# Attention pairs 4 and 5 moved to the padded, DMA-transposed form in a fused state-space and gated-FFN kernel

## The chip, the cores and the metric

The kernel runs on one core of one Trainium2 chip. The metric is the device time of one launch in microseconds (us), taken as the median of several runs. TensorE multiplies matrices, VectorE and ScalarE empty its results from PSUM, GpSimd works on SBUF alone, and SyncE issues most of the DMAs. In the profile they are PE (PEld for its weight loads), DVE, ACT, POOL and SP. An engine with a small q behind its name is its instruction queue, which issues DMAs.

## The reference

Two layers stand behind each other. The first is a chunked state-space attention over 4 batches, 8 heads, 768 positions, head width 32 and state width 16:

```python
# per batch and head, chunk by chunk
cum = cumsum(log a);  L = exp(cum_i - cum_j), causal
y  = ((C @ B.T) * L) @ x          # inside a chunk ("intra")
y += exp(cum) * (C @ state)       # from earlier chunks ("inter")
state = decay * state + sum_j B_j x_j * decay_from_j
```

The second takes `y` as 3072 tokens of width 256 through a gated FFN with 1536 hidden columns: `out = (relu(y @ w_gate) * (y @ w_val)) @ w_out`. Inputs and output are float32; the kernel multiplies in bfloat16.

## The kernel before

The attention works on 12 pairs of 128-position chunks (three pairs to a batch), the FFN on 6 blocks of 512 tokens. Block b of the FFN needs pairs 2b and 2b+1. While block b is computed, the attention of the next two pairs, called P = 2b+2 and Q = 2b+3 in the code, is slipped between its matmuls; W = 2b+1 is the pair before. The order on every engine is the order of the text: `in_order` ties each instruction to the one before it on its engine, so an engine that waits holds up all that stands behind it in the text.

A pair goes through these steps. `load_bc` and `load_x` issue its DMAs from SP: C, B and x, two DMAs each. GpSimd scales B and C by the decays and casts x (`to_x`). TensorE needs B and C with positions along the free axis. Then come the scores (`G`, `G_rows`), which ScalarE, VectorE and GpSimd copy out and mask (`gevac`; `causal` is GpSimd's part of the mask, on what ScalarE has copied), the product of the scores with x (`Dm`, `Dm_two`), the part from earlier chunks (`inter`, `inter_rows`) and the copy of both to `yT`, from which the FFN reads. The chunk states are built up in one PSUM tile, `A_ps`.

There are three forms of a pair:

- Pairs 0 to 3 are "wide": the even and odd positions of a chunk pair are interleaved. `scale_bc` writes B and C to `bs`, TensorE transposes them (`turn`), ScalarE and VectorE copy the result (`tevac`).
- Pairs 4 and 5 (`p < NDMA`, line 283) go through `scale_bc` and `turn` as well, without the interleaving. Their states come from `states` and `spread`, which keep a state in a 128x256 masked form `Sm` for one matmul of full height.
- Pairs 6 to 11 are "padded": `scale_padded` writes B and C with zeros between into one of three buffers `bz`, and SP issues a DMA transpose into `TT`. TensorE does nothing for it. States come from `states_two` for two pairs at once and are summed by `sums_two` (VectorE adds, GpSimd makes the masked copy `Sn`); `inter_rows` multiplies them in tiles of 32 rows.

The FFN part of a block has 12 hidden slices. `gv` computes one for 512 tokens, `gvh` for 256 at a time: the second half of a block's tokens comes from pair W, and a block can start on the first half before pair W is done. The number of slices done in halves is `nh`: 4 in block 0 (ahead of the loop), 6 in block 1, 8 in block 2, none later. In the middle of the halves for the first 256 tokens stands pair W's last part. Then `fout` multiplies the 12 slices by `w_out` for four groups of 128 tokens (`ts` 0 to 3), and the attention of P and Q goes between these.

For blocks 2 and later the stretch of `fout` holds, in this order on TensorE: 9 slices, `G_rows(P)`, both `inter_rows`, 16 more slices, `G_rows(Q)`, 19 slices, `Dm_two((P, Q))`, `states_two` of the two pairs after, 4 slices.

Of the kernel before, what the change touches and what calls it, by code (L numbers as in the profile page):

```python
# [8 lines left out]
FP32 = mybir.dt.float32  # L9
# [20 lines left out]
def kernel(  # L30
# [70 lines left out]

    def load(p, q):
# [12 lines left out]
    even = const.tile([128, 24], FP32)  # L115
# [137 lines left out]
    over2 = const.tile([128, NB], FP32)  # L253
# [6 lines left out]
    def over_sum(de):  # L260
        own = smask.rearrange("p t (q d) -> p (t q) d", q=4)[:, :, 0]
        prod = const.tile([128, NB, 8], FP32)
        nc.vector.tensor_tensor(
            out=prod, in0=de.rearrange("p (b h) -> p b h", b=NB),
            in1=own.rearrange("p (o h) -> p o h", o=1).to_broadcast([128, NB, 8]),
            op=ALU.mult)
        nc.vector.tensor_reduce(out=over, in_=prod, op=ALU.add, axis=mybir.AxisListType.X)

    def over_sum2(de):
        own = smask.rearrange("p t (q d) -> p q t d", q=4)[:, :, :, 0]  # L270
        prod = const.tile([128, 2, 8], FP32)
        for n in range(2):
            nc.vector.tensor_tensor(
                out=prod[:, n].rearrange("p (q t) -> p q t", t=2),
                in0=de[:, (2 + n) * 8:(3 + n) * 8].rearrange("p (q t) -> p q t", t=2),
                in1=own, op=ALU.mult)
        nc.vector.tensor_reduce(out=over2[:, 2:4], in_=prod, op=ALU.add,
                                axis=mybir.AxisListType.X)
# [4 lines left out]
    NDMA = 6  # L283
# [8 lines left out]
    def scale_padded(p, eng):  # L292
# [11 lines left out]
        st[p]["B"] = [z[:, 4 * i] for i in range(2)]  # L304
        tt = st[p]["TT"] = att.tile([128, 8, 128], BF16, tag="TT", name="TT", bufs=4)
        nc.sync.dma_start_transpose(out=tt, in_=z.rearrange("s k n -> s (k n)"))

    def new_bs(p):
        st[p]["bs"] = att.tile([128, 4, 128], BF16, tag="bs", name="bs", bufs=6)
        bs = st[p]["bs"]  # L310
        if p < NWIDE:
            st[p]["tin"] = [[bs[:, 2 * j + r] for r in range(2)] for j in range(2)]
        else:
            st[p]["tin"] = [[bs[:, 2 * i + j] for i in range(2)] for j in range(2)]
            st[p]["B"] = st[p]["tin"][0]
# [4 lines left out]
    def views(p, js):  # L320
        s = st[p]
        dst = s["bs"].rearrange("s k (q t n) -> s k t q n", q=4, t=2)
        if p < NWIDE:
            ks = slice(2 * js.start, 2 * js.stop)
            src = s["bcr"].rearrange("s (t q) j r n -> s (j r) t q n", t=2)
            return src[:, ks], dst[:, ks]
        return s["bcr"].rearrange("s i j (t q) n -> s (i j) t q n", t=2), dst

    def cast_bc(p, eng, js):
        src, dst = views(p, js)  # L330
        for t in range(2):
            copy(eng, dst[:, :, t], src[:, :, t])

    def scale_bc(p, eng, js=slice(0, 2), f=None, ts=(0, 1)):
        b, c0, _ = place(p)
        src, dst = views(p, js)
        if f is None:
            if p < NWIDE:
                f = wfac[:, p, js].rearrange("s j r h -> s (j r) h")
            else:  # L340
                f = fac[:, b, c0:c0 + 2].rearrange("s c j h -> s (c j) h")
        n = f.shape[1]
        for t in ts:
            eng.tensor_tensor(  # L344
                out=dst[:, :, t], in0=src[:, :, t],
                in1=f[:, :, 4 * t:4 * t + 4].to_broadcast([128, n, 4, N]), op=ALU.mult)

    def scale_one(p, eng, j):

        b, c0, _ = place(p)  # L350
        for i in range(2):
            f = fac[:, b, c0 + i, j].rearrange("s (t q) -> s t q", t=2)
            eng.tensor_tensor(
                out=st[p]["bs"][:, 2 * i + j].rearrange("s (q t n) -> s t q n", q=4, t=2),
                in0=st[p]["bcr"][:, i, j].rearrange("s (t q) n -> s t q n", t=2),
                in1=f.to_broadcast([128, 2, 4, N]), op=ALU.mult)

    def to_x(p, eng, f=None):
        xb = att.tile([128, 2 * NH * D], BF16, tag="xb", name="xb", bufs=6)
        xr = st[p]["xr"].rearrange("s i h d -> s (i h) d")  # L360
        out = xb.rearrange("s (k d) -> s k d", d=D)
        if f is None:
            copy(eng, out, xr)
        else:
            eng.tensor_tensor(out=out, in0=xr, in1=f.to_broadcast([128, 2 * NH, D]),
                              op=ALU.mult)
        st[p]["x"] = [xb[:, i * NH * D:(i + 1) * NH * D] for i in range(2)]

    def scale(p, eng):
        if p >= NDMA:  # L370
            scale_padded(p, eng)
        else:
            new_bs(p)
            scale_bc(p, eng)
        to_x(p, eng)
# [15 lines left out]
    def bevac(p, eng):  # L391
# [3 lines left out]
        if p < NWIDE:  # L395
            src = src.rearrange("s r m -> s m r")
            dst = dst.rearrange("s (m r) -> s m r", r=2)
        else:
            src = src.rearrange("s i m -> s (i m)")
        copy(eng, dst, src)  # L400
# [16 lines left out]
    def ct(p, i, rows=slice(0, 128), t=None):  # L417
        if p < NWIDE:
            c = st[p]["CT"][rows, :, :, 64 * i:64 * i + 64]
        else:  # L420
            c = st[p]["CT"][rows, :, i]
        return c if t is None else c[:, t]

    def split(p, ap):

        return ap.rearrange("s t (r m) -> s t r m", r=2) if p < NWIDE else ap
# [17 lines left out]
    def G(p):  # L444
# [4 lines left out]
        for i in range(2):  # L449
            for q in range(4):  # L450
                r = slice(32 * q, 32 * q + 32)
                nc.tensor.matmul(  # L452
                    out=split(p, g[q][:, i]), lhsT=s["BT"][r, i], rhs=ct(p, i, r),
# [100 lines left out]
    chunks = {}  # L554

    def states(p):
        c0 = 2 * (p % PPB)
        last = c0 + 2 == NC
        chunks[p] = (st[p]["B"], st[p]["x"])
        todo = [(0, p, 0)]  # L560
        if c0 and not last:
            todo.insert(0, (0, p - 1, 1))
        if not last:
            todo += [(1, p, 0), (1, p, 1)]
        for n, (k, e, i) in enumerate(todo):
            B_, x_ = chunks[e]
            xi = x_[i].rearrange("s (t q d) -> s q t d", t=2, q=4)
            for q in range(4):
                nc.tensor.matmul(
                    out=A_ps[0][32 * q:32 * q + 32, 0, 64 * k:64 * k + 64].rearrange(  # L570
                        "p (t d) -> p t d", t=2),
                    lhsT=B_[i][:, 32 * q:32 * q + 32], rhs=xi[:, q],
                    start=(n == 0 and (c0 == 0 or last)), stop=True,
                    tile_position=(0, 32 * q),
                    skip_group_check=True)

    def spread(p):
        for k in range(1 if 2 * (p % PPB) + 2 == NC else 2):
            S[2 * p + k + 1] = spread_one(2 * p + k + 1, k)

    def y_bank(s, apart=False):
        if "y" not in s:
# [4 lines left out]
            else:  # L587
                y = mm.tile([128, 2, 2, 128], FP32, tag="y", name="y")
                s["y"] = [y[:, 0], y[:, 1]]
                s["ya"] = y  # L590
# [8 lines left out]
    def inter(p, i):  # L599
# [5 lines left out]
        for t in range(2):  # L605
# [10 lines left out]
            out = s["y"][t][:, i]  # L616
            if p < NWIDE:
                out = out.rearrange("s (r m) -> s r m", r=2)
            nc.tensor.matmul(  # L619
                out=out, lhsT=Sm[:, t], rhs=ct(p, i, t=t),  # L620
# [16 lines left out]
    def yevac(p, *engs):  # L637
        s = st.pop(p)
        dst = yT[:, :, p * 256:(p + 1) * 256]
        if p >= NWIDE:  # L640
            copy(engs[0], dst.rearrange("q t (i m) -> q t i m", i=2), s["ya"])
            return
# [14 lines left out]
    def inter_rows(p, opened):  # L657

        for i in range(2):
# [3 lines left out]
            for q in range(4):  # L663
# [5 lines left out]
                opened.add(q)  # L669

# [29 lines left out]
    def sums_two(ps):  # L700

        A = A_ps[0].rearrange("p a d -> p (a d)")
        for n, (p, i) in enumerate(todo(ps)):
            c = 2 * p + i
# [96 lines left out]
    def foevac(b, ts, o=None):  # L801
# [10 lines left out]
        rows = out[r0 - 128:r0 + 128, :].rearrange("(i p) m -> p i m", p=128)  # L812
        for part in ((slice(0, 1), slice(1, 2)) if b in (2, 3) and ts == 3 else (slice(0, 2),)):
            nc.sync.dma_start(out=rows[:, part], in_=ob[:, part])
# [116 lines left out]
    de = const.tile([128, BH], FP32)  # L931
# [21 lines left out]
    nc.scalar.copy(out=de, in_=de_ps)  # L953
# [9 lines left out]
    for b in range(NBLK):  # L963
        P, Q, W = 2 * b + 2, 2 * b + 3, 2 * b + 1
        more = P < NPAIR
        if b == 1:
            load(P + 2, nc.sync)
            load(P + 3, nc.sync)
        if b == 2:
            scale(Q, nc.gpsimd)  # L970
            load(Q + 2, nc.sync)

        nh = (4, 6, 8, 0)[min(b, 3)]
        for f in range(nh):
            if b == 0:
                continue
            turning = f == (3 if b == 1 else nh - 3)
# [3 lines left out]
            if b == 1 and f == 1:  # L981
                to_x(P, nc.scalar)
            if turning:
                inter(W, 0)
                inter(W, 1)
                Dm(W)
                if b == 1:
                    states(P)
# [167 lines left out]
```

## Time and profile before

| | |
|---|---|
| median of 3 runs (lowest to highest) | 122.64 us (122.54 to 122.77) |
| the profiled execution's own time | 122.54 us |
| its span in the profile | 120.8 us |
| PE busy in the span | 116.8 us (97%) |
| DVE, ACT, POOL busy | 89.2, 74.3, 51.4 us |
| DMA queue of SP (q1) | 73088 packets, 10.54 MB |
| DMA transposes (`TT<-bz`) | 6, median 3.9 us from issue to landing |

The page gives each engine's busy time and, in 40 slices of the span, its share in tenths. The chain of waits goes back from the last instruction to what released it. Times in a timeline are us from the start of the span; `x2` means two instructions merged to one row, and the square bracket names the idle time of the engine ahead of the row and what ended it. 1.74 us of the profiled execution lie outside the span.

### The profile page before, as it was taken

What the parts mean: (1) busy time and instruction counts of PE and PEld (TensorE: products, weight loads), DVE (VectorE), ACT (ScalarE), POOL (GpSimd) and SP (SyncE); (2) the same over time, 40 slices, a digit from 0 to 9 for tenths busy, and PEclk for the clock granted to TensorE, in tenths of its full rate; (3) what the DMA queues carried; (4) which work ended last, traced back from release to release, by engine and by line L of the source; (5) the groups of instructions that cost most, each with busy time, mean ns of one, the idle gap of its engine ahead of it and who ended that gap; (6) DMA issues with size and microseconds to landing.
All of it is one profiled execution on the core that took longest, in us unless ns stands there. A gap on an engine that the chain in (4) does not pass through costs nothing.

```text
span 120.8 us, 3330 instructions
## 1 busy us (share of the span) xinstructions
PE 116.8 (97%) x1238; PEld 75.1 (62%) x1238; DVE 89.2 (74%) x214; ACT 74.3 (61%) x161; POOL 51.4 (43%) x104
## 2 busy tenths in 40 slices
PE   7999999999999999999999999999999999999990
PEld 2446854577885477888487544578444677444790
DVE  5898879986999956899875687856778675678500
ACT  4077886752998734888734767526767445766240
POOL 6879999741805342957076273333400033000000
PEclk9999999999999999999999999999999999999999
DMA  2999999999998999999986799962200002200022
GB/s 57 215 186 176 192 173 197 211 144 127 159 125 151 133 101 109 121 242 134 98 148 121 84 122 149 194 130 82 91 5 0 0 0 92 87 0 0 0 87 87
DMA packets 80591, 13.69 MB, mean 113 GB/s; under 512 B 73424, under 2 KB 80576, under 8 KB 80576
## 3 DMA queue, kind: packets, MB, share of 16 engines
q1 hardware_dynamic: 73088, 10.54, 58.5%
q0 software_dynamic: 4080, 2.36, 14.1%
q10 hardware_dynamic: 3408, 0.59, 2.6%
q8 instruction: 9, 0.15, 0.5%
q14 instruction: 6, 0.05, 0.1%
HBM read 11.12 MB, written 3.15 MB: 118 GB/s over the span
## 4 chain that ended last, share of the span: by engine, by line
PE 94%; DVE 3%; ACT 0%; issue 0%; DVEq 0%
PE o L783 26%; PE gate L738 19%; PE val L738 19%; PE gv L753 13%; PE w L200 3%; PE g L452 2%; PE g L491 2%; PE y L678 1%; PE y L630 1%; PE o L795 1%; PE tp L389 1%; DVE gs L475 1%; DVE bs L344 1%; PE y L619 1%; PE y L665 0%; PE dw L236 0%
## 5 line engine op out<-in xcount | busy, mean ns | idle before, releaser
L742 DVE TENSOR_TENSOR h<-r,val 128x512 bf16<-128x512 bf16 x54 | 36.7, 687 | 9.3 <-ACT r L741 6.4
L741 ACT ACTIVATE r<-gate 128x512 bf16<-128x512 f32 x54 | 32.2, 597 | 11.9 <-PE gate L738 10.9
L783 PE MATMUL o<-wo,h 128*128 128x256 bf16 x276 | 33.6, 273 | 0.0
L738 PE MATMUL val<-yT,wv 128*128 128x512 bf16 x108 | 32.6, 379 | 0.0
L738 PE MATMUL gate<-yT,wg 128*128 128x512 bf16 x108 | 32.6, 379 | 0.0
L783 PEld LDWEIGHTS <-h 128*128 128x128 bf16 x276 | 25.8, 98 | 5.5 <-issue 1.2
L171 POOL TENSOR_SCALAR_AFFINE_SELECT gs<-gs 128x512 bf16<-128x512 bf16 (+1 forms) x24 | 12.2, 533 | 24.9 <-ACT gs L464 24.9
L475 DVE TENSOR_TENSOR gs<-g,masks 128x512 bf16<-128x512 f32 x24 | 15.4, 685 | 5.9 <-PE g L491 2.8
L738 PEld LDWEIGHTS <-wv 128*128 128x128 bf16 x108 | 10.6, 98 | 12.5 <-DMA wv<-in_moe_w_val_dram 0.2
L738 PEld LDWEIGHTS <-wg 128*128 128x128 bf16 x108 | 10.4, 98 | 11.1
L464 ACT CAST gs<-g 128x512 bf16<-128x512 f32 x12 | 7.0, 587 | 14.7 <-PE g L452 6.4
L763 DVE TENSOR_TENSOR h<-r,gv 128x256 bf16<-128x256 bf16 x36 | 13.9, 417 | 0.9 <-ACT r L760 0.7
L760 ACT ACTIVATE r<-gv 128x256 bf16<-128x256 f32 x36 | 13.7, 389 | 1.2
L753 PE MATMUL gv<-yT,wg 128*128 128x256 bf16 x72 | 13.9, 273 | 0.0
L753 PE MATMUL gv<-yT,wv 128*128 128x256 bf16 x72 | 13.9, 272 | 0.0
L297 POOL TENSOR_TENSOR bz<-bcr,fac 128x512 bf16<-128x512 f32 x6 | 6.4, 1059 | 10.5 <-DMA bcr<-in_B_dram 10.5
L811 ACT COPY ob<-o 128x512 f32<-128x512 f32 x11 | 6.5, 592 | 4.1 <-PE o L783 4.0
L318 ACT CAST yT<-y 128x512 bf16<-128x512 f32 (+1 forms) x9 | 4.6, 531 | 5.4 <-PE y L678 3.4
L753 PEld LDWEIGHTS <-wv 128*128 128x128 bf16 x72 | 7.0, 98 | 0.8
L753 PEld LDWEIGHTS <-wg 128*128 128x128 bf16 x72 | 6.8, 98 | 1.1 <-issue 0.2
L200 PE MATMUL w<-const-bfloat16-1.0 128*128 128x512 bf16 (+3 forms) x16 | 6.0, 497 | 0.8 <-PEq L1140 0.8
L318 DVE CAST yT<-y 128x256 bf16<-128x256 f32 (+1 forms) x7 | 3.7, 548 | 4.0 <-PE y L678 2.0
(119 smaller groups left out, 112.0 us busy)
## 6 DMA issues: line engine op xcount, KB each, us to landing
xr<-in_x_dram SPq DMA_DIRECT2D x23, 128.0 KB, 3.2
out_dram<-ob SPq DMA_DIRECT2D x9, 256.0 KB, 2.7
bcr<-in_B_dram SPq DMA_DIRECT2D x16, 64.0 KB, 3.0
bcr<-in_C_dram SPq DMA_DIRECT2D x16, 64.0 KB, 2.9
wg<-in_moe_w_gate_dram POOLq DMA_DIRECT2D x6, 128.0 KB, 5.0
wv<-in_moe_w_val_dram POOLq DMA_DIRECT2D x6, 128.0 KB, 5.1
wo<-in_moe_w_out_dram POOLq DMA_DIRECT2D x3, 256.0 KB, 7.1
out_dram<-ob SPq DMA_DIRECT2D x4, 128.0 KB, 2.3
```

Of the source, the lines that this page charges most:

```text
L171: nc.gpsimd.affine_select(out=dst, in_=dst, pattern=pattern, compare_op=ALU.is_ge, fill=0.0, base=0, channel_multiplier=-1)
L200: nc.tensor.matmul(out=w[:, 0:cols], lhsT=nc.const_aps.tensor(1.0, [128, 128], BF16), rhs=nc.const_aps.tensor(1.0, [128, cols], BF16), sta ...
L318: (eng.copy if eng is nc.scalar else eng.tensor_copy)(out=out, in_=in_)
L464: nc.scalar.copy(out=d[:, 0], in_=g[0])
L475: nc.vector.tensor_tensor(out=d[:, q], in0=g[q], in1=m, op=ALU.mult)
L738: nc.tensor.matmul(out=o, lhsT=w_tile(ws, f, k), rhs=yT[:, k, tk], start=(k == 0), stop=(k == 1), skip_group_check=True)
L741: nc.scalar.activation(r, g, AF.Relu)
L742: nc.vector.tensor_tensor(out=fst[b][:, f], in0=r, in1=v, op=ALU.mult)
L753: nc.tensor.matmul(out=gv_[:, j], lhsT=w_tile((wgs, wvs)[j], f, k), rhs=yT[:, k, tk], start=(k == 0 and not (early and j)), stop=(k == 1), ...
L760: nc.scalar.activation(r[:, 0:256], fst[b, f, u][:, 0], AF.Relu)
L763: nc.vector.tensor_tensor(out=fst[b][:, f, u * 256:(u + 1) * 256], in0=fst.pop((b, f, u, "r"))[:, 0:256], in1=fst.pop((b, f, u))[:, 1], op ...
L783: nc.tensor.matmul(out=o[:, ts % 2], lhsT=fst[b][:, f, ts * 128:(ts + 1) * 128], rhs=wo[:, f], start=(f == 0 and new), stop=(f == NF - 1), ...
```

## The change

Pairs 4 and 5 get the padded form of pairs 6 to 11, so that two more DMA transposes are issued and TensorE no longer transposes these pairs. Pair 3 stays wide but takes its heads in natural order, as the padded pairs do, so that its states can go through `states_two` and `sums_two`; two new functions, `inter_wide` and `yevac_wide`, do its last part. Block 1 takes the order that block 2 had (8 slices in halves, pair W's part behind the sixth), and block 2 the order of the later blocks (no halves). States of pairs 4 and 5 are computed behind slice 8 of block 1; those of pairs 6 and 7 follow `Dm_two((4, 5))` in block 1, where in the old kernel they stood in block 2. The product of the old running sum with the decay goes from GpSimd to VectorE. The two DMAs of C of pair 5 are issued by ScalarE instead of SP. B and C of pairs 6 and 7 are issued ahead of both their x, and ScalarE casts these two x (`to_x`) between its copies of the scores of pairs 4 and 5.

```diff
+    def load_part(p, j=None, q=nc.sync):
+        if j is not None:
+            ...
+            load_bc(p, j, q)
+            return
+        new_x(p)
+        for i in range(2):
+            load_x(p, i, q)
...
-    NDMA = 6
+    NATURAL = 3
...
+    def turn_padded(p):
         tt = st[p]["TT"] = att.tile([128, 8, 128], BF16, tag="TT", name="TT", bufs=4)
-        nc.sync.dma_start_transpose(out=tt, in_=z.rearrange("s k n -> s (k n)"))
+        nc.sync.dma_start_transpose(out=tt, in_=turned[p % 3].rearrange("s k n -> s (k n)"))
...
+    def inter_wide(p, i, opened):
+        Sm = S.pop(2 * p + i)
+        for t in range(2):
+            for q in range(4):
+                r, o = slice(32 * q, 32 * q + 32), 64 * (q % 2)
+                nc.tensor.matmul(
+                    out=Y[q // 2][o:o + 64, p % 2, i].rearrange("s (r m) -> s r m", r=2),
+                    lhsT=Sm[r], rhs=ct(p, i, r, t=t), start=q not in opened, stop=True,
+                    tile_position=(32 * q, o), skip_group_check=True)
+                opened.add(q)
...
-                nc.gpsimd.tensor_scalar_mul(past, total, over2[:, c // NC:c // NC + 1])
+                nc.vector.tensor_scalar_mul(past, total, over[:, c // NC:c // NC + 1])
...
         if b == 1:
-            load(P + 2, nc.sync)
-            load(P + 3, nc.sync)
-        if b == 2:
-            scale(Q, nc.gpsimd)
-            load(Q + 2, nc.sync)
-        nh = (4, 6, 8, 0)[min(b, 3)]
-        for f in range(nh):
-            if b == 0:
-                continue
-            turning = f == (3 if b == 1 else nh - 3)
+            scale_padded(Q, nc.gpsimd)
+            turn_padded(Q)
+            to_x(P, nc.gpsimd)
+            to_x(Q, nc.gpsimd)
+            load_part(Q + 2, 1)
+            load_part(Q + 2, 0)
+            load_part(P + 2)
+            load_part(Q + 2)
+            scale_padded(P + 2, nc.gpsimd)
+        nh = (4, 8, 0)[min(b, 2)]
+        for f in range(nh if b else 0):
             gvh_mm(b, f, 0)
             gvh_relu(b, f, 0)
             gvh_mul(b, f, 0)
...
+            if f == 5:
+                opened = y_banks()
+                inter_wide(W, 1, opened)
+                Dm_two((W,))
+                yevac_wide(W, nc.scalar, nc.vector)
...
             elif b == 1:
-                if f == nh:
-                    turn(P)
-                    tevac(P, nc.scalar, nc.vector)
-                    scale(Q, nc.gpsimd)
                 if f == 8:
-                    turn(Q)
-                    tevac(Q, nc.scalar, nc.vector)
-                    scale(Q + 1, nc.gpsimd)
-                    load(Q + 3, nc.sync)
+                    states_two((P, Q))
+                sums_two((P, Q), (f - 8,))
+                if f == 11:
+                    scale_padded(Q + 2, nc.gpsimd)
+                    turn_padded(P + 2)
+                    turn_padded(Q + 2)
+                    load(P + 4, nc.sync)
+                    load(Q + 4, nc.sync)
...
             foevac(b, 1)
             to_x(Q, nc.scalar)
+            load_part(Q + 2, 1, nc.scalar)
             fout(b, 2)
             state(P, 0)
             state(P, 1)
-            held(Q + 2)
+            load_part(Q + 2, 0)
+            load_part(Q + 2)
             back(Q)
...
+            Dm(P)
+            states_two((Q,))
+            scale_padded(Q + 1, nc.gpsimd)
+            turn_padded(Q + 1)
+            yevac(P, nc.vector)
+            G(Q)
+            gevac(Q, after={3: lambda: sums_two((Q,))})
+            load_part(Q + 3, 1)
+            load_part(Q + 3, 0)
...
             gevac(P)
+            if b == 1:
+                to_x(P + 2, nc.scalar)
...
             foevac(b, 1, first_two)
+            if b == 1:
+                to_x(Q + 2, nc.scalar)
```

In the order of the built program, SP's queue from the loads of pair 4 on is then: C4, B4, x4, output of tokens 0 to 255, B5, x5, transpose of pair 4, C6, B6, output of tokens 256 to 511, transpose of pair 5, C7, B7, x6, x7, transposes of pairs 6 and 7, the loads of pair 8 (each letter two DMAs). Before it was: B4, x4, C4, output, C5, B5, x5, output, C6, B6, x6, C7, B7, x7, transpose of pair 6, the loads of pair 8.

More of the change, by code (lines that the diff above doesn't have):

```diff
@@ L345, in scale_bc, with to_x @@
                 out=dst[:, :, t], in0=src[:, :, t],
[L346 to L358, printed above, removed]
-        xb = att.tile([128, 2 * NH * D], BF16, tag="xb", name="xb", bufs=6)
[L360 to L366, printed above, removed]
+                in1=f[:, :, t].to_broadcast([128, n, 4, N]), op=ALU.mult)
+    def to_x(p, eng):
+        xb = att.tile([128, 2 * NH * D], BF16, tag="xb", name="xb", bufs=6)
+        copy(eng, xb.rearrange("s (k d) -> s k d", d=D),
+             st[p]["xr"].rearrange("s i h d -> s (i h) d"))
         st[p]["x"] = [xb[:, i * NH * D:(i + 1) * NH * D] for i in range(2)]
     def scale(p, eng):
[L370 to L374, printed above, removed]
+        scale_padded(p, eng)
+        turn_padded(p)
         to_x(p, eng)
@@ L550, in spread_one @@
         return n
[L554 to L579, printed above, removed]
     def y_bank(s, apart=False):
@@ L669, in inter_rows, with yevac_wide @@
                 opened.add(q)
+    def inter_wide(p, i, opened):
[8 more added lines that the diff above has]
+                opened.add(q)
+    def yevac_wide(p, *engs):
+        for k in range(2):
+            copy(engs[k], yT[:, k, p * 256:(p + 1) * 256].rearrange(
+                     "q (i m r) -> q i r m", i=2, r=2),
+                 Y[k][:, p % 2].rearrange("q i (r m) -> q i r m", r=2))
+        st.pop(p)
     def Dm_two(ps):
@@ L811, in foevac @@
         nc.scalar.copy(out=ob, in_=o or fst["o"])
-        rows = out[r0 - 128:r0 + 128, :].rearrange("(i p) m -> p i m", p=128)
-        for part in ((slice(0, 1), slice(1, 2)) if b in (2, 3) and ts == 3 else (slice(0, 2),)):
-            nc.sync.dma_start(out=rows[:, part], in_=ob[:, part])
+        nc.sync.dma_start(
+            out=out[r0 - 128:r0 + 128, :].rearrange("(i p) m -> p i m", p=128), in_=ob)
     B_, C_ = slice(0, 1), slice(1, 2)
```

156 lines of the change are left out of this document (33 added, 123 removed).

## The prediction

> **What bounds the kernel now.** I read the page's busy times and slices first, then the chain of waits in order of time, then the timelines of SP's queue, ScalarE and GpSimd.
>
> The page: PE is busy for nearly the whole span, and from the second slice to the last but one none is below nine tenths. The DMA engines are almost as full up to about slice 26, that is 79 us.
>
> ```profile
> PE 116.8 (97%) x1238; PEld 75.1 (62%) x1238; DVE 89.2 (74%) x214; ACT 74.3 (61%) x161; POOL 51.4 (43%) x104
> PE   7999999999999999999999999999999999999990
> DMA  2999999999998999999986799962200002200022
> ```
>
> The chain in order of time is PE on PE: no other engine's piece stands in it between 11 and 118 us. So time is saved by taking work off PE, and lost where something that PE needs comes late. These pieces mark the starts of blocks 1 to 4 and the costs used below.
>
> ```profile
> 30.78 1.86 PE gv L753 x16
> ...
> 32.76 0.34 PE y L630 x16
> ...
> 42.44 0.22 PE y L619 x4
> ...
> 49.14 2.62 PE gv L753 x24
> ...
> 61.70 0.17 PE y L665 x12
> ...
> 66.25 0.56 PE y L678 x32
> ...
> 67.44 0.21 PE gate L738
> ...
> 84.88 0.22 PE gate L738
> ```
>
> The timeline of SP's queue shows the second resource without slack. From 36.20 to 44.60 us, 12 loads follow each other without an idle stretch, one each 0.70 us. Two transposes stand in this queue among copies.
>
> ```profile
> 36.20 1.18 SPq L92 DMA_DIRECT2D bcr<-in_C_dram  x2
> 37.43 1.35 SPq L92 DMA_DIRECT2D bcr<-in_B_dram  x2
> 38.87 1.18 SPq L100 DMA_DIRECT2D xr<-in_x_dram  x2
> ...
> 44.60 1.41 SPq L306 DMA_TRANSPOSE TT<-bz  x1
> 46.06 2.26 SPq L92 DMA_DIRECT2D bcr<-in_C_dram  x2
> 48.36 1.53 SPq L92 DMA_DIRECT2D bcr<-in_B_dram  x2
> 49.99 1.39 SPq L100 DMA_DIRECT2D xr<-in_x_dram  x2
> ```
>
> **PE's own work.** Block 2 of the new kernel has the contents of block 3 of the old: 12 full slices, two `G_rows`, 12 `inter_rows` matmuls, `Dm_two`, 12 state matmuls. Old block 3 lasts 84.88 - 67.44 = 17.44 us. New block 1 is old block 2 (67.44 - 49.14 = 18.30) with these edits: pair W's `inter` goes from 4 matmuls of full height (0.22) to 8 small ones (8/12 of 0.17 = 0.11), -0.11; its `Dm` goes from 0.34 to half of 0.56, -0.06; the 16 state matmuls there (0.12) go, -0.12; four more `inter_rows` matmuls (the fourth chunk; 16 take 0.22 in block 4), +0.05; four more state matmuls behind `Dm_two`, +0.03; 12 state matmuls alone behind slice 8. No row shows state matmuls between two slices. Their bounds are 0.09 (12/16 of 0.12) and 0.35 (the same with the 0.2 to 0.25 by which a short group costs more between slices, as the 8-matmul `G` does with 0.33); I take the upper one, the nearest in kind. Sum: 18.30 - 0.11 - 0.06 - 0.12 + 0.05 + 0.03 + 0.35 = 18.44. Block 0 loses 4 state matmuls, -0.03. Old blocks 1 and 2 take 18.36 + 18.30 = 36.66, new ones 18.44 + 17.44 = 35.88: -0.78, with block 0 -0.81 us. The lower bound of the one unknown would make it -1.07. In this the 8 transposes (0.22 for 4) of pairs 4 and 5 and their four large `inter` matmuls each (0.22) are gone. Without any new wait the profiled 122.54 would become 121.73, and the median of 122.64 about 121.8.
>
> **Edits that cost nothing.** VectorE takes three products by the old sum (0.28 each, the `carry` row of line 538) and loses the masked states (0.42 each) and four copies of C in block 1; it is 74% busy. One more small product in `over_sum` falls in block 0, where PE waits for nobody. ScalarE's two issues for C5 take some 0.6 us each by its own DMA issues at the start; they fall into the 2.24 us it idles ahead of 30.10. Were that cover gone, `gevac(3)` would move by 1.2 us and `Dm_two((3,))` with it. ScalarE loses two copies of B and wins one cast.
>
> **The queue of SP.** Here the change puts two transposes (pairs 4 and 5) ahead of B, C of pair 7 and x of pairs 6 and 7, and takes two loads out (C5). In the old kernel the queue is through with x7 at 44.60. What does a transpose cost there? From 44.60 to 49.99 one transpose and four loads take 5.39 us; from 36.20 to 38.87 four loads alone take 2.67. The transpose costs 2.72. The next, at 52.62, costs 3.22 by the same sum (the x of its group starts at 58.51). The pair at 75.52, with no load behind it, takes 2.96 for both, so 1.48 is the floor: SP's own time for one. I take 2.0, nearer to the floor, since both larger readings hold a slow stretch that the 44.60 holds too (33 to 36 us, loads of 1.2 us instead of 0.6) and that would otherwise be counted twice. The queue then reaches the end of x7 at 44.60 - 2 x 0.70 + 2 x 2.0 = 47.2. The second DMA of x6 is three issues earlier, 45.1, and lands 3.0 later (median for x in this stretch), at 48.1 us. The second DMA of B7 is issued at 43.7 and lands at 46.7.
>
> Who waits for these? In the new block 1 the states of pairs 6 and 7 stand 0.6 us ahead of its end: 30.78 + 18.44 - 0.6 = 48.6 us. In the old kernel they stood at 52.3.
>
> - ScalarE's cast of x6 is queued right behind `gevac(4)`, at about 44.1. ScalarE stands there until 48.1, and behind it are queued: the two copies of pair 5's scores, the output copy, the cast of x7. With these rows the cast and the copies follow at steps of 0.50, 0.48, 0.27 and 0.50, and the cast of x7 takes 0.62: x7 is ready at 50.5.
>
> ```profile
> 32.15 0.61 ACT L318 CAST xb<-xr 128x512 bf16<-128x512 f32 x1
> ...
> 44.38 0.59 ACT L464 CAST gs<-g 128x512 bf16<-128x512 f32 x1 [1.74 <-PE g L452]
> 44.86 0.38 ACT L472 CAST gs<-g 128x256 bf16<-128x256 f32 x1
> ```
>
> - GpSimd's `scale_padded(7)` stands ahead of the masks of pairs 4 and 5. It starts at 46.7, ends 1.65 later (1.06 + 0.06 + 0.53, the rows at 41.26 and 42.38), and the masks follow at 0.5 each, those of pair 5 behind ScalarE's copies at 49.2 and 49.6: the last at 50.3, for a `Dm_two` that PE would reach at 48.0.
>
> Both end close together; the cast ends last. PE waits for 50.5 + 0.1 - 48.6 = 2.0 us in `Dm_two((4, 5))` and the states behind it. What follows is not late: by then the remaining loads have 10 us until `G_rows(6)`.
>
> At the rate at which the DMA engines, and not SP, were the limit, C5's move would bring nothing, and the -1.40 for it would fall away. The Trainium skill ("Trainium Kernel Development and Optimization", Key Constraints) says that issuing from several engines only saves the sequencer's issue time, as all share the DMA engines. By it the sum would end 1.4 later only if SP's time is not what counts; SP's rows above, with issue after issue, speak for SP.
>
> **Sum.** 122.54 - 0.81 + 2.0 = 123.73 for the profiled execution, 123.8 beside the median of 122.64.
>
> **Rivals.**
>
> *The transfers come in time* (faster). If a transpose took a plain load's 0.70, x6 would land at 48.1 - 2 x 1.3 = 45.5 and x7 1.4 later. ScalarE would stand until 45.5 only, have x7 cast at 47.9, and GpSimd's last mask would come at 47.7; no wait is left, and the time is 121.8. The point from which it decides is x6 landing at 46.1. For it: the quickest transpose in the trace lands after 2.7 us, as a load does. Against it: 2.72 and 3.22, and even the floor of 1.48 lands x6 at 47.1. The Trainium skill ("Advanced Engine Details and Errata", X-Bar Transpose) says that transposes are as fast as regular DMAs on this chip; by that rule this rival wins. This trace doesn't bear it out: 3.9 us median to landing, against 3.0 for loads.
>
> *The DMA engines are the limit* (slower still). Then C5 through ScalarE takes their time all the same, x6 lands 1.4 later: 125.2. The share of nine tenths in the DMA row is for it, the steady issues are against it.
>
> *An earlier wait at pair 3's part.* `scale_padded(4)` stands ahead of pair 3's masks on GpSimd. B4 would land at 30.2, the scaling ends at 31.8, masks at 32.9, the first state copy (0.3) at 33.2, against PE at 33.5. From 0.3 us of delay on it costs up to 0.6; it is lost in the later wait where there is one (that ends at a DMA's time), and makes the first rival 122.4.
>
> **How the numbers follow.** Late transfers with SP as the limit: 0.59, with a range of its own from 122.8 (transposes at 1.48, wait 1.0) to 125.3 (at 2.72, wait 3.4). DMA engines as the limit: 0.10. In time: 0.25, at 121.8. In time but with the earlier wait, or late by a few tenths: 0.06. A measurement of this kernel can tell about 0.2% (0.25 us) from no change. Faster by more: 0.25; within: 0.07; slower by more: 0.68. The range reaches from the first rival, 121.7, to 125.3.
>
> **What would show it.** In the new profile: block 2 of 17.4 us; an idle PE of 1 to 3.4 us in `Dm_two` and its states near 48 to 51 us; ScalarE idle ahead of an `xb` cast, released by the x DMA; GpSimd's `bz` behind B7. SP's queue should show 2 us a transpose near 33 and 40. I am wrong if the loads of x6 land by 46.1, or if PE idles before 40 us for more than 0.6.

## The result: slower by 2.5%, and the profile after

The changed kernel takes 126.34 us (median of 4, 124.88 to 128.32) where the kernel before took 122.70 on the same chip (4 runs, 122.54 to 122.79). The ratio is 1.025, with an interval of 1.021 to 1.029. The prediction was 123.8 us with a range up to 125.3: the sign and the chain of waits were right, the time lies outside the range. The profiled execution takes 126.68 us, its span 125.0; that is 4.14 more than the 122.54 of before. Here and below a ratio is taken over the fast runs of both kernels, those within 1.5% of the fastest, and a median over all runs.

The page first. PE's busy time hardly moves (116.8 before), but its slices now have gaps: 8 and 7 from 25 to 31 us, ahead of block 1, an 8 from 44 to 47 and a 4 from 50 to 53 us. (The two 8s before 9 us cost nothing: the first `gv` matmul starts at 10.01 us in both kernels.) The granted clock stays full in this execution.

```profile
PE 116.4 (93%) x1217; PEld 71.9 (58%) x1224; DVE 88.2 (71%) x204; ACT 72.9 (58%) x151; POOL 51.8 (41%) x106
PE   7889999987999989499999999999999999999991
PEclk9999999999999999999999999999999999999999
DMA  3999999989998987989799999960220002200022
```

The chain in order of time (start, length, what) was PE on PE before. Now, from 14 to 53 us, it runs through a load of B (pair 3), GpSimd, SP's queue issue after issue, another load of B (pair 7, landing at 49.22), GpSimd's scaling of that pair (`bz`) and the masks behind it. Only then does PE go on.

```profile
14.20 10.25 DMA bcr<-in_B_dram
24.60 1.21 POOL bs L330 x2
...
34.99 1.13 SPq L310
...
41.96 1.29 SPq L310
43.30 0.57 SPq L92
43.92 0.57 SPq L92
44.54 0.66 SPq L92
45.24 3.98 DMA bcr<-in_B_dram
49.44 1.07 POOL bz L299
50.56 0.53 POOL bz L305 x2
51.08 1.92 POOL gs L181 x4
53.04 0.43 PE y L619 x17
```

ScalarE's timeline shows the second predicted queue. It stands for 4.15 us ahead of the cast of x6, which landed at 50.69. Behind the cast come the copies of pair 5's scores, the output copy and the cast of x7, which ends at 53.16.

```profile
50.77 0.62 ACT L317 CAST xb<-xr 128x512 bf16<-128x512 f32 x1 [4.15 <-DMA xr<-in_x_dram]
51.29 0.58 ACT L420 CAST gs<-g 128x512 bf16<-128x512 f32 x1
51.77 0.38 ACT L428 CAST gs<-g 128x256 bf16<-128x256 f32 x1
52.03 0.60 ACT L754 COPY ob<-o 128x512 f32<-128x512 f32 x1
52.53 0.63 ACT L317 CAST xb<-xr 128x512 bf16<-128x512 f32 x1
```

PE's timeline has the two places where it waits in block 1: ahead of `fout` for the sums of pairs 4 and 5 (L651), and in `Dm_two((4, 5))` (L619).

```profile
44.15 1.16 PE L726 MATMUL o<-wo,h 128*128 128x256 bf16 x9 [0.48 <-DVE run L651]
...
51.72 0.60 PE L619 MATMUL y<-gs,xb 128*32 128x128 bf16 x8 [1.32 <-POOL gs L181]
52.68 0.82 PE L619 MATMUL y<-gs,xb 128*32 128x128 bf16 x24 [0.36 <-POOL gs L181]
```

The table by block (time; then busy us of PE, PEld, DVE, ACT, POOL with instruction counts; granted clock; DMA share; GB/s) closes the sum.

```profile
32.09:54.00 21.91, 19.55 (x261) 14.12 (x261) 15.21 (x37) 13.50 (x31) 11.41 (x25) 1.00 1.05 144
54.00:71.44 17.44, 17.39 (x186) 10.34 (x185) 13.01 (x25) 10.55 (x19) 7.53 (x16) 1.00 0.93 136
```

Before, blocks 1 and 2 started at 30.74 and 48.97 and ended at 67.28, by the first matmul of each: 18.23 + 18.31 = 36.54. Now they take 21.91 + 17.44 = 39.35, which is 2.81 more, and block 1 starts 1.35 later: 4.16 us, the whole difference. Block 2 takes exactly the 17.44 that was predicted. So all of the loss lies before 54 us.

Of the late start, 1.06 us are two waits of PE for GpSimd, which stands behind the load of B of pair 3 that took 10.25 us to land:

```profile
25.87 0.40 PE L357 MATMUL tp<-ident,bs 128*128 128x128 bf16 x4 [0.41 <-POOL bs L330]
...
29.09 0.21 PE L465 MATMUL A_ps<-xb,bx 128*32 128x64 bf16 x4 [0.65 <-POOL xb L317]
```

Within block 1, against the same stretches of the old block 2 and of a kernel of the new form that does not wait in blocks 1 and 2 (the last variant below), `fout` starts 0.6 late, the first `G_rows` with both `inter_rows` takes 0.15 longer and `Dm_two` with its states 2.5 longer: 3.25. What is left of the 21.91 is 18.66.

### The profile page after: what moved, and what is told of

It reads as the page before. It is cut to its first block, busy times and chain, and to the rows that moved or that the text cites. A ratio compares the mean times of both kernels' runs of the same rounds, so it can differ in the third digit from the quotient of the medians.

```text
span 125.0 us, 3282 instructions
## 1 busy us (share of the span) xinstructions
PE 116.4 (93%) x1217; PEld 71.9 (58%) x1224; DVE 88.2 (71%) x204; ACT 72.9 (58%) x151; POOL 51.8 (41%) x106
## 3 DMA queue, kind: packets, MB, share of 16 engines
q0 software_dynamic: 4080, 2.36, 13.4%
## 4 chain that ended last, share of the span: by engine, by line
PE 57%; DMA 14%; SPq 12%; POOL 9%; DVE 4%; issue 2%; ACT 0%; POOLq 0%; DVEq 0%
PE gate L681 17%; PE o L726 17%; PE val L681 16%; DMA bcr<-in_B_dram 11%; SPq L92 5%; SPq L86 3%; DMA bcr<-in_C_dram 3%; POOL gs L181 2%; POOL bz L291 2%; SPq L310 2%; POOL bz L299 2%; PE g L447 2%; PE y L619 2%; PE o L738 1%; DVE bs L330 1%
## 5 line engine op out<-in xcount | busy, mean ns | idle before, releaser
L685 DVE TENSOR_TENSOR h<-r,val 128x512 bf16<-128x512 bf16 x60 | 40.7, 686 | 10.2 <-ACT r L684 7.6
L684 ACT ACTIVATE r<-gate 128x512 bf16<-128x512 f32 x60 | 35.8, 597 | 14.0 <-PE gate L681 13.1
L681 PEld LDWEIGHTS <-wv 128*128 128x128 bf16 x120 | 11.7, 98 | 13.9 <-DMA wv<-in_moe_w_val_dram 0.7
L681 PEld LDWEIGHTS <-wg 128*128 128x128 bf16 x120 | 11.6, 98 | 12.9
L706 DVE TENSOR_TENSOR h<-r,gv 128x256 bf16<-128x256 bf16 x24 | 9.4, 416 | 0.7 <-ACT r L703 0.5
L703 ACT ACTIVATE r<-gv 128x256 bf16<-128x256 f32 x24 | 9.2, 388 | 1.0 <-PE gv L696 0.2
L696 PE MATMUL gv<-yT,wg 128*128 128x256 bf16 x48 | 9.3, 273 | 0.0
L696 PE MATMUL gv<-yT,wv 128*128 128x256 bf16 x48 | 9.3, 273 | 0.0
L660 POOL TENSOR_TENSOR Sn<-run,tmask 128x64 bf16<-128x64 f32 x15 | 4.1, 293 | 6.3 <-DVE run L651 3.9
L435 DVE TENSOR_TENSOR gs<-g,masks 128x256 bf16<-128x256 f32 x11 | 4.6, 415 | 2.5 <-ACT gs L428 2.5
```

The lines of the kernel that those rows point to most:

```text
L681: nc.tensor.matmul(out=o, lhsT=w_tile(ws, f, k), rhs=yT[:, k, tk], start=(k == 0), stop=(k == 1), skip_group_check=True)
L684: nc.scalar.activation(r, g, AF.Relu)
L685: nc.vector.tensor_tensor(out=fst[b][:, f], in0=r, in1=v, op=ALU.mult)
L696: nc.tensor.matmul(out=gv_[:, j], lhsT=w_tile((wgs, wvs)[j], f, k), rhs=yT[:, k, tk], start=(k == 0 and not (early and j)), stop=(k == 1), ...
L703: nc.scalar.activation(r[:, 0:256], fst[b, f, u][:, 0], AF.Relu)
L706: nc.vector.tensor_tensor(out=fst[b][:, f, u * 256:(u + 1) * 256], in0=fst.pop((b, f, u, "r"))[:, 0:256], in1=fst.pop((b, f, u))[:, 1], op ...
```

## Experiments

Two theories stood after the result. *Queue*: the transposes of pairs 4 and 5 delay B7 and x6 in SP's queue, and that decides. *DMA engines*: these are full, C5's move to ScalarE brings nothing, and loads are late with or without the transposes. Each group of runs stood beside runs of the kernel before on the same chip, whose medians were 122.70 us (the result), 123.14 (`e1_again` to `e4_late_states`), 123.42 (`e5_best` to `e8_no_turn_clean`) and 122.69 (`e9_inter_late`, `e10_before`); across groups only the ratios can be compared.

**The same kernel again** (`e1_again`, no edit).

> The changed kernel as it is, for its profile and its spread. In the first profile block 1 started at 32.10 us instead of 30.78, because B of pair 3 landed at 24.44 instead of 18.96. If this lateness belongs to the program, block 1 starts near 32.1 again and the profiled execution takes 126 to 127 us. If it belongs to one execution, block 1 starts near 30.8 and the time is 124.9 to 125.3. Both theories expect PE idle for 2 to 3 us in Dm_two of pairs 4 and 5.

Measured: 126.70 us, ratio 1.028 (1.021 to 1.034). Its profiled execution (126.95 us) has nearly the time of the first, from other pieces. In the table of PE's waits (engine, line, waited for: us in total, times, longest) pair 3's wait, of which the first profile had nothing at this place, is 1.3, the wait for the sums 1.3, and the wait in `Dm_two` 0.9.

```profile
PE o L726 <- DVE run L651: 1.3, 1, 1.3
PE y L599 <- POOL Sn L660: 1.3, 1, 1.3
PE y L619 <- POOL gs L181: 0.9, 1, 0.9
```

PE arrives later at `Dm_two` and waits less there, since what it waits for comes at a DMA's time: x6 landed at 51.03 here and at 50.69 in the first profile. Adding up waits therefore does not explain the time of these two; the end of the last one does.

Block 1 started at 31.47, between the two expectations. Over the ten profiles of the changed kernel and its variants it started from 30.62 to 32.09, in the two of the kernel before at 30.74 and 31.30. So most of the first profile's late start belongs to that execution, and with a start 0.6 earlier the time was no shorter.

**No transposes for pairs 4 and 5** (`e2_no_turn`). The scores then come from a weight tile instead of the transposed B and C.

```diff
     def turn_padded(p):
+        if p < 6:
+            st[p]["TT"] = wo[:, 0:4].rearrange("s f (k n) -> s (f k) n", n=128)
+            return
```

> The DMA transposes of pairs 4 and 5 are left out (their scores are computed from w_out's tile instead). Theory of late loads: the two transposes cost SP's queue 3.7 and 1.4 us, so x6 and B7 land about 5 us earlier, near 45.7 and 44.3, the wait in Dm_two falls from 2.65 us to under 0.2, and what is left over the sum of PE's work is the 0.6 us of fout waiting for the PSUM tile of the sums: 122.4 us, or 123.7 with the late start of block 1. Rival, that the new order on ScalarE and GpSimd holds TensorE whatever the loads do: 125 us or more still.

Measured: 124.47 us, ratio 1.006 (1.002 to 1.011), 2.2 us less than `e1_again`. x6 landed at 47.05 instead of 51.03, B7 at 45.00 instead of 48.66: 3.98 and 3.66 us for two transposes, near the 2 x 2.0 of the prediction and less than the 5 us expected. The time is 0.8 us above the expected 122.4 to 123.7, and below the rival's 125. The timeline of SP's queue shows loads without a gap where the transposes stood, and no wait is left in `Dm_two`; what remains are pair 3's 1.0 and 0.5 for the sums.

```profile
36.42 2.75 SPq L92 DMA_DIRECT2D bcr<-in_B_dram  x2
39.27 0.53 SPq L758 DMA_DIRECT2D out_dram<-ob  x1
39.89 1.19 SPq L92 DMA_DIRECT2D bcr<-in_C_dram  x2
41.13 1.84 SPq L92 DMA_DIRECT2D bcr<-in_B_dram  x2
43.07 2.98 SPq L100 DMA_DIRECT2D xr<-in_x_dram  x4
```

What the prediction had wrong shows too: by its sum x6 lands at 48.1 with the transposes, so 44.1 without. It lands about 3 us later than that in both kernels: the base of the queue was off.

The ten profiles of the changed kernel and its variants say more on the price of a transpose. From the second issue of x5 to the second of B7, between which both transposes stand or don't, SP took 9.96 to 11.27 us with them (8 profiles, mean 10.59) and 7.88 and 8.08 without: 2.6 us for both, 1.3 each. Counted from the same issue of x5, B7 lands 3.5 us and x6 2.2 us later with them, on average. So the single pair of profiles above lies on the high side, and only two profiles stand without transposes.

**C of pair 5 issued by SP again** (`e3_c5_sp`).

```diff
-            load_part(Q + 2, 1, nc.scalar)
+            load_part(Q + 2, 1)
```

> One part undone: C of pair 5 is issued by SP again. If SP's own issue time sets the pace, two more issues put x6 and B7 1.3 us later and the time 1.0 to 1.4 us above e1_again. If the DMA engines set the pace, the time is the same within 0.3 us. If the two issues on ScalarE cost more than they bring, it is faster.

Measured: 127.73 us, ratio 1.036 (1.028 to 1.044), which overlaps that of `e1_again`. The median is 1.0 us above `e1_again`, as the first theory expected. But two of the four runs have a mean granted clock of 0.987, in `e1_again` one of four; the other two took 126.60 and 127.03, against 125.67 to 126.95 there. So the time does not decide, and the landings must. x6 landed at 50.74, against 51.03 with C5 on ScalarE; B7 at 49.41, against 48.66 there and 49.22 in the first profile. Neither is the 1.3 us of the first theory: moving C5 did not bring x6 forward, and B7 by 0.75 or 0.19 us, where the two executions of the changed kernel differ by 0.56. From the second issue of x3 to the second of x5, between which C5 stands or doesn't, SP takes 9.83 us on average with C5 on ScalarE (9 profiled executions, 8.98 to 10.69) and 10.16 with C5 on SP (this one and both of before, 9.65 to 10.69): 0.3 us won, within the scatter, not the predicted 1.40. The rule that the prediction weighed (the Trainium skill, "Trainium Kernel Development and Optimization", Key Constraints: issuing from several engines only saves issue time, the DMA engines are shared) agrees with these traces as far as the scatter lets one tell. The rival built on it had 0.10.

Its longer profiled execution (128.5 us) has another cause. The table by stretches shows the clock (column 1.00 or 0.51) at half for 3.4 us right behind the wait, in which PE was busy 2.36 of 4.40 us; block 2 takes 18.49 us instead of 17.44:

```profile
49.00:53.40 4.40, 2.36 (x40) 1.57 (x42) 1.03 (x3) 2.48 (x5) 3.50 (x7) 1.00 0.93 160
53.40:56.80 3.40, 3.40 (x43) 1.77 (x32) 1.75 (x6) 1.69 (x3) 1.13 (x4) 0.51 0.88 121
```

**States of pairs 6 and 7 in block 2** (`e4_late_states`): they follow slice 4 of block 2, x6 and x7 are cast by GpSimd at that block's start, `scale_padded(7)` stands behind the masks of pair 5. The diff shows the main moves; the others are named in the expectation.

```diff
+        if b == 2:
+            to_x(P, nc.gpsimd)
+            to_x(Q, nc.gpsimd)
...
+                if b == 2 and f == 4:
+                    states_two((P, Q))
+                    sums_two((P, Q))
...
-            ahead = (P + 2, Q + 2) if Q + 2 < NPAIR else ()
+            ahead = (P + 2, Q + 2) if Q + 2 < NPAIR and b > 1 else ()
```

> Only the places are changed: states and sums of pairs 6 and 7 behind slice 4 of block 2, their x cast by GpSimd at the start of block 2, scale_padded of pair 6 behind the sums of pairs 4 and 5 and that of pair 7 behind the masks of pair 5, and all three sums of pairs 4 and 5 right behind their states. Theory of late loads: nothing waits for x6, x7 or B7 before 56 us, so Dm_two's wait and that of fout for the sums both go: 122.54 - 0.81 + 0.2 (one more lone group of state matmuls) = 121.9 us, or 123.2 with the late start of block 1. Rival, that the form itself is dearer on PE than my count: above 122.5 with block 1 starting at 30.8.

Measured: 129.40 us, ratio 1.043 (1.034 to 1.053): missed. The wait in `Dm_two` is gone as expected, but a longer one came in block 2. In the table of waits PE stands 3.1 us for `h`, VectorE's timeline says why: it waits 3.62 us for GpSimd's masked copies `Sn`, which in this order are queued behind the scaling of pair 8, and that waits for its loads (B8 landed at 57.28, its scaling started at 57.44). Another 1.1 us is the wait at pair 3's part.

```profile
PE val L681 <- DVE h L685: 3.1, 1, 3.1
PE y L599 <- POOL Sn L660: 1.1, 1, 1.1
```

```profile
60.53 0.27 DVE L656 TENSOR_SCALAR run<-run,over 128x64 f32<-128x64 f32 x1 [3.62 <-POOL Sn L660]
```

The stretches around it show the same half clock, here for 5.9 us behind 3.1 us without a matmul:

```profile
58.30:61.40 3.10, 0.00 (x0) 0.00 (x0) 0.87 (x3) 0.60 (x1) 2.34 (x8) 0.86 0.91 91
61.40:67.30 5.90, 5.86 (x14) 2.08 (x14) 3.23 (x5) 1.73 (x3) 2.14 (x4) 0.50 1.01 195
```

**One early wait taken away at a time.** `e6_sums` puts three sums right behind the states of pairs 4 and 5, so that `fout` doesn't wait for them; `e7_mask3` puts `scale_padded(4)` behind pair 3's masks.

```diff
# e6_sums
-                sums_two((P, Q), (f - 8,))
+                    sums_two((P, Q))
# e7_mask3
-            scale_padded(Q + 1, nc.gpsimd)
-            turn_padded(Q + 1)
             yevac(P, nc.vector)
             G(Q)
             gevac(Q, after={3: lambda: sums_two((Q,))})
+            scale_padded(Q + 1, nc.gpsimd)
+            turn_padded(Q + 1)
```

> The changed kernel with one edit: the three sums of pairs 4 and 5 right behind their states, so that fout finds its PSUM tile free. If the waits add, it gains the 0.5 to 1.3 us that fout waited. If the wait in Dm_two ends at the landing of B7 and x6 whenever TensorE comes there (theory of late loads), that wait grows by as much, and the time is the changed kernel's within 0.4 us.

> The changed kernel with one edit: on GpSimd, scale_padded of pair 4 goes behind the masks and the state copies of pair 3. The wait of inter_wide for the state copy (0.4 to 1.3 us near 34) goes. Theory of late loads: the transpose of pair 4 is issued up to 1 us later, x6 and B7 land as late or later, and the wait in Dm_two takes what was won: 0 to 0.8 us slower than the changed kernel. If the waits add, 0.4 to 1.3 us faster.

Measured: 127.69 us, 1.034 (1.028 to 1.039), and 126.93 us, 1.029 (1.024 to 1.034). Neither gains. By the ratios `e6_sums` is 0.6% above `e1_again`, some 0.7 us where 0.4 was expected at most; the intervals overlap, and two of its four runs have a granted clock of 0.986 and 0.987. `e7_mask3` is 0.1% above, as expected. In its profile pair 3's wait is gone and the wait in `Dm_two` is 2.1 us:

```profile
PE y L619 <- POOL gs L181: 2.1, 2, 1.7
PE o L726 <- DVE run L651: 0.5, 1, 0.5
```

The profile of `e6_sums` has 1.7 us in `Dm_two`, 1.2 at pair 3's part and no wait for the sums. Block 1 ends at 54.59 in `e6_sums` and at 53.71 in `e7_mask3`, against 54.00 and 54.28 in the two profiles of the changed kernel. So an earlier wait is lost in the later one, as the prediction's third rival said.

**Both of these and no transposes** (`e8_no_turn_clean`).

> The transposes of pairs 4 and 5 left out (scores from w_out's tile instead), and both edits of e6 and e7 made. If late loads and these two queues are all that the change costs, PE is dense and shows its own work alone: 121.7 to 122.0 us, block 1 of 18.4 and block 2 of 17.4 us. If a wait is left in block 1 or 2, there is a further cause.

Measured: 123.61 us (10 runs), ratio 0.999 (0.996 to 1.003). The expected 121.7 to 122.0 is missed. Beside the 1.034 and 1.029 of the two runs before it, which have the transposes, it shows a second time that the loss goes with them. The profiled execution (125.31, its longest) still waits 1.3 us in `Dm_two`: B7 landed at 46.10 and x6 at 49.25 there, without any transpose ahead of them, against 45.00 and 47.05 in `e2_no_turn`. Between these two executions the same loads differ by 1.1 and 2.2 us, and this place in block 1 has no room for that.

**The repaired order** (`e5_best`: `e4` with `scale_padded(4)` behind pair 3's masks and the scaling of pairs 8 and 9 behind slices 6 and 9; `e9_inter_late`: the same with pair 5's `inter_rows` behind its own `G_rows`).

```diff
# e5_best, against e4_late_states
-                if f in (2, 6):
-                    scale(P + 2 + f // 4, nc.gpsimd)
+                if f in ((6, 9) if b == 2 else (2, 6)):
+                    k = int(f > (6 if b == 2 else 2))
+                    scale(P + 2 + k, nc.gpsimd)
# e9_inter_late, against e5_best
-            inter_rows(Q, opened)
+            if b > 1:
+                inter_rows(Q, opened)
...
+            if b == 1:
+                inter_rows(Q, opened)
```

> e4_late_states with its two queues mended: scale_padded of pair 4 stands behind the masks and state copies of pair 3 on GpSimd, and in block 2 the scaling of pairs 8 and 9 stands behind slices 6 and 9, so that the state copies of pairs 6 and 7 don't queue behind the loads of pair 8. Theory: every wait found so far (pair 3's part 1.1 us, fout for the sums, Dm_two, block 2's 3.1 us with the half clock behind it) is one of a queue, not of the form; then PE is dense from 31 us on and the time is 122.54 - 0.81 + 0.2 = 121.9 us, a ratio of 0.994 to before. Rival: the two transposes bring the loads of pairs 8 to 11 behind their need as well; then PE idles in blocks 2 or 3 and the time is above 123.

> e5_best with one more edit: in block 1 the inter_rows of pair 5 goes behind its G_rows, because in e5_best TensorE stood 0.83 us there for the transpose of pair 5, which landed at 44.80 us, while G_rows of pair 5 comes at 46. Theory: the last wait of block 1 goes, 0.8 to 1.0 us faster than e5_best, a ratio of 0.992 to 0.995 to before. Rival: the transpose lands later in most executions than in the one profiled, and the wait moves to G_rows: no gain over 0.3 us.

Measured: `e5_best` 123.57 us (12 runs), ratio 1.001 (0.998 to 1.004); the expected 0.994 is missed. Its profile has one wait of PE from block 1 on, for the transpose of pair 5, which `inter_rows(5)` needs as much as `G_rows(5)` does, but 2 us earlier:

```profile
44.85 0.30 PE L587 MATMUL y<-TT,Sn 32*64 32x128 bf16 x8 [0.83 <-DMA TT<-bz]
```

`e9_inter_late` takes 122.49 us (12 runs, 122.25 to 123.29), ratio 0.9985 (0.9965 to 1.0005), with no wait of PE in blocks 1 and 2. By the two ratios it is 2.6% faster than the changed kernel and no faster than the kernel before, as far as 12 runs can tell. The expected 0.992 to 0.995 is missed: against `e5_best` the ratio fell by 0.25%, about the 0.3 us that the rival allowed, with intervals that overlap. Its table by block:

```profile
30.98:49.54 18.56, 18.51 (x244) 13.85 (x244) 15.18 (x37) 12.45 (x29) 11.79 (x25) 1.00 0.93 146
49.54:67.32 17.78, 17.68 (x199) 10.44 (x200) 12.85 (x25) 10.54 (x19) 8.59 (x19) 1.00 0.93 148
```

18.56 + 17.78 = 36.34, against 36.54 before: all that the new form saves in this order, once nothing waits, is 0.2 us, or 0.16%.

**The kernel before once more** (`e10_before`), to see how its queue varies.

> The kernel before, for a second profile. The queue of SP in the changed kernels issued the last DMA of x5 at 34.0 to 35.0 us, where the slots of the old queue put it at 32.4 to 33.0. If the old kernel's first profile was a lucky execution, its loads of pair 3 and 4 are 0.5 to 1.5 us later here too, with TensorE still dense. If the lateness belongs to the changed program, its queue stands as in the first profile.

Measured: 122.74 us (8 runs), ratio 1.000. As the first theory expected, its queue is late too, with TensorE dense. In this execution block 1 starts at 31.30 instead of 30.74, and SP's queue is 0.9 us later than in the profile that the prediction was made from: the transpose of pair 6 is issued at 45.49, not 44.60.

```profile
42.65 1.33 SPq L92 DMA_DIRECT2D bcr<-in_B_dram  x2
44.02 1.37 SPq L100 DMA_DIRECT2D xr<-in_x_dram  x2
45.49 1.41 SPq L306 DMA_TRANSPOSE TT<-bz  x1
```

PE has no gap for it in blocks 1 and 2 (they take 18.23 + 18.31 again): in the old order nobody needs x7 before 52.3 us.

## Why the prediction was right and wrong

*What bounds the kernel, and the mechanism: right.* Before, PE; after, the chain SP's queue, B7, GpSimd's scaling, the masks, `Dm_two`, with ScalarE's stand at x6 ending beside it (last mask 53.00, last cast 53.16; predicted 50.3 and 50.5). That the transposes cause the loss is shown by `e2_no_turn` and `e8_no_turn_clean`; that what comes after is not late, by block 2's 17.44.

*Two transposes at 2.0 each: right in one pair of profiles (3.98 and 3.66 together), too much for SP's queue by all of them* (1.3 each). The prediction expected 2 us a transpose in SP's rows; from the issue of a transpose to the next issue they show 1.52 and 1.34.

*The landing of B7 and x6: wrong, and this is the step that failed.* The term is "The queue then reaches the end of x7 at 44.60 - 2 x 0.70 + 2 x 2.0 = 47.2", from which x6 followed at 48.1 and B7 at 46.7. Measured: 50.69 and 49.22, 2.6 and 2.5 later. For B7, which ends the chain, the excess has two parts.

The first is the base of the queue: B7's second DMA was issued at 45.24 instead of 43.7, 1.5 late. That much was there before the first of the new transposes: x5's second issue came at 33.97, where the sum has 33.61 - 1.40 = 32.21. Of these 1.76 us, 1.03 stood already at the second issue of x3, ahead of C5's place in the queue (24.99, against 23.96 in the profile that the sum was made from). The second profile of the kernel before is 0.67 later than the first there, and 1.15 later at x5 (34.76). The other 0.73 is the credit for C5: from x3 to x5 SP took 0.67 less than in that profile (8.98 instead of 9.65) and not 1.40, and on average 0.3 less. That the rest of the queue added nothing more is a balance of errors: the loads between x5 and B7 took longer than priced, the transposes less.

The second part is the landing. B7 took 3.98 us instead of 3.0, another 1.0. The 3.0 was a median over loads of x; this load of B stands behind a transpose in a full queue. With the transposes it takes 3.2 to 4.8 us (8 profiles, mean 3.9), without them 2.9 and 3.2; the second load of x6 shows no such difference (3.4 to 4.1, against 3.0 and 4.9). So for B7 the longer landing goes with the transposes, and why stays open.

With the end of the last mask at 53.0 instead of 50.3, the sum 123.73 + 2.7 becomes 126.4, against 126.68.

*PE's own saving: the size was off, by 0.3.* Predicted 0.78 for blocks 1 and 2. Without waits block 1 would take 18.6 and block 2 17.44 (the last variant's 18.56 + 17.78, with one group of states moved back from slice 4 to behind `Dm_two`): 36.05, so 0.5 is saved. The lone states behind slice 8 cost 0.30, near the upper bound of 0.35 that was taken. Pair W's part was over-credited: from the end of slice 6's first half to the next slice takes 0.67 instead of 0.78 in the old block 2, a gain of 0.11 where 0.29 was summed from single rows. And the old blocks' 36.66, read from marks of the chain, was 36.54 by the first matmul of each.

*A wait that was not foreseen.* `fout` shares its PSUM tiles with the states' sums, and stood 0.5 to 1.3 us for VectorE's last read of them (L651). The prediction costed the sums by VectorE's load alone, not by who waits for the buffer. The same goes for `inter_rows(5)` ahead of `G_rows(5)`. The first was hidden in the later wait here; the second shows in `e5_best`, with 0.83 us.

*The rivals.* "Transfers in time" fell: B7 and x6 are late, and a transpose costs SP's queue some 1.3 us, a load 0.7. A transpose moves 256 KB, a load 64 or 128, so the nearer comparison is with the outputs of 256 KB: in the changed kernel's rows from 30 to 42 us they hold SP for 0.81 and 0.83 us and the transposes for 1.47 and 1.29, and the medians to landing are 2.7 and 3.9 us. So the rule that transposes are as fast as regular DMAs (the Trainium skill, "Advanced Engine Details and Errata", X-Bar Transpose) is not borne out in this queue.

"DMA engines are the limit" was near: it put the issue of B7 at 43.7 + 1.4 = 45.1, and it came at 45.24; the landing was missing. Part of that is luck, since 1.03 us of the lateness stood ahead of C5's place. The rival had 0.10 because issue after issue in SP's rows was read as SP being the limit. C5's small gain speaks against that reading; that full DMA engines hold SP up is argued from the DMA row of nine tenths, not shown by a run. "Pair 3's part" was under-priced (up to 0.6; measured 0 to 1.3) and, as it said, absorbed.

*The signs.* Idle time of PE of more than 0.6 us before 40 us was named as a sign of being wrong, and it came: 1.06 us ahead of block 1 in the first profile, 1.28 at pair 3's part in `e1_again`. It did not decide, since the loads set the end of block 1 in both (54.00 and 54.28).

*The range* was made from the price of the transpose alone. It took the base of the queue as given, from one profiled execution that turned out to be an early one. In hindsight, with C5 at 0.3 and the queue 1.15 later, as in the second profile of the kernel before, the same sum gives 123.73 + 1.1 + 1.15 = 126.0. The 0.3 of PE's saving does not come on top, since the wait ends at a load's time.

## What to carry to other kernels

Where the DMA row is near full, price an issue that is moved to another engine's queue near nothing until a trace shows the loads behind it earlier: here it won 0.3 of 1.40 us. A sum that ends at a transfer's time hangs on that transfer's whole lateness; take the base from two profiles, or widen the range by what they differ. And when work is moved earlier, list what each moved step reads and which buffer it holds, and who is queued behind it: of the five waits that came up in these kernels, four were a buffer, an input or a place in GpSimd's queue that no busy time shows.

## What was not expected of the hardware

PE's granted clock can halve in a wait, and the half clock costs extra. It stood at 0.50 for 5.9 us after 3.1 us without a matmul (`e4_late_states`): block 2 took 23.98 us there and 17.78 in `e9_inter_late`, which has the same matmuls in it, so that the clock cost about as much again as the wait. It stood at 0.51 for 3.4 us after a stretch in which PE was busy 2.36 of 4.40 us (`e3_c5_sp`, with waits of 1.53 and 0.36). The length of the wait alone does not decide: at the same place `e7_mask3` waited 1.75 and 0.36 us and the changed kernel's own profiled execution 1.32 and 0.36, and both kept 1.00. The Trainium skill ("TensorE: Matmul & The Clock Gate", Part 1) gives an idle window of about 3.4 us; here a slightly shorter pause was enough.

The clock is part of the changed kernel's spread. Its 4 runs spread over 3.4 us, where the 4 runs of the kernel before beside them spread over 0.25; the longest, 128.32, has a mean granted clock of 0.987, the other three 0.997 and more. Of the 24 runs of the changed kernel and `e1_again`, `e3_c5_sp`, `e4_late_states`, `e6_sums` and `e7_mask3`, 10 have a granted clock of 0.973 to 0.987; of the 44 runs of `e2_no_turn`, `e5_best`, `e8_no_turn_clean` and `e9_inter_late`, none is below 0.99. Without the longest, the changed kernel still spreads over 1.8 us. Transfers vary between executions, as SP's queue shows above; that this makes the 1.8 us is argued, not shown.
